# A 64-row product made a 128-row product in the spatial step of a gated MLP

## The chip, the cores and the metric

The program runs on one core of one Trainium2 chip. The metric is the device time of one execution, in microseconds; a kernel's time is the median of several runs.

## What is computed

The program chains three blocks over 4 batches of 576 positions and 512 channels: an attention with a window of 64 positions, an MLP on a Fourier-mixed input, and a gated MLP (gMLP) with a spatial product. Only the last block touches the change. In the reference it reads, cut to what matters:

```python
def _moe2_ref(x, w_in, g_ln, w_sg, b_sg, w_out):
    h = x @ w_in                      # 512 -> 1024 channels
    h = gelu_tanh(h)
    u, v = h[..., :512], h[..., 512:]
    v_n = (v - mean(v)) / np.sqrt(var(v) + 1e-06) * g_ln
    v_s = np.einsum('ts,bsd->btd', w_sg, v_n) + b_sg[None, :, None]
    return x + (u * v_s) @ w_out
```

The spatial product is the `einsum`: for each batch a 576 x 576 matrix over positions times a 576 x 512 matrix.

## The kernel before, in words

Every float32 operand is split into a high part with few mantissa bits and a low part, and a product is made as three matmuls that accumulate in one PSUM tile: high by high, high by low, low by high. The helper `mm3` records these three (L118, L119, L120) for each K tile of 128 rows. Because it is a helper, most matmuls of the program carry its three lines.

The gMLP runs last. `gate_u` makes the half u for all batches. Then for each batch b there are three steps on TensorE, in this order: `spatial(b)`, the spatial product; `v_tiles(b + 1)`, which makes and normalises the half v of the next batch with positions on partitions; `project(b)`, which multiplies the gated result by `w_out` and adds the residual. TensorE runs them back to back, and what it does in `v_tiles` and `project` gives VectorE and ScalarE time to finish the operands of the next `spatial`.

576 positions are four K tiles of 128 and a rest of 64. `spatial` works through two halves h of the output positions (320 and 256 columns) and four groups c of 128 channels, so 8 PSUM tiles for each batch and 32 in all. Each gets 14 matmuls: 4 times the three of `mm3`, and two for the rest of 64 positions. For that rest the tile `vtail[o]` (128 rows by 512 channels) holds the high part of the 64 positions in one half of its rows and the low part in the other half; for even b the high part is in rows 0 to 63, for odd b in rows 64 to 127. The rest's weights, `sg[4, h]`, are stored with the same 64 rows twice, so both halves of the rows hold the same numbers; `sh` is the high part, `sl` the low part. One matmul of 128 rows (L706) thus gives high by high and low by high at once. A second one (L707) gives high by low: only the 64 rows with the high part, chosen by `hr`.

When a tile's last matmul is done, VectorE reads it (L710), multiplies by u (L711), ScalarE rounds to the high part `xh` (L712), and VectorE makes the low part `xl` (L713). The intermediate `dec_w` has two buffers. PSUM has eight tiles for this stage: six of the tag `c` and two of the tag `g`, which `ctile` hands out in turn.

The order on each engine is fixed when the program is built, by a scheduler. In the first batch it puts five of the L706/L707 pairs one behind the other; in the three other batches each pair stands behind the 12 matmuls of its tile.

Of the kernel before, what the change touches and what calls it, by code (L numbers as in the profile page):

```python
# [41 lines left out]
EPS = 1e-6  # L42
# [2 lines left out]


def split(a):
    """float64 -> two float32 arrays: one with 11 mantissa bits, and the rest."""
    u = a.astype(np.float32).view(np.uint32).astype(np.uint64)
    u = (u + 0x7FF + ((u >> 12) & 1)) & 0xFFFFF000  # L50
    hi = u.astype(np.uint32).view(np.float32)
    return hi, (a - hi.astype(np.float64)).astype(np.float32)
# [49 lines left out]
class Kernel:  # L102
# [8 lines left out]
        return p, es  # L111

    def mm3(self, out, terms, first=True, last=True):
        """out += sum over terms of (lh + ll) @ (rh + rl) without ll @ rl."""
        n = len(terms)
        for i, (lh, ll, rh, rl) in enumerate(terms):
            mm = self.nc.tensor.matmul
            mm(out, lhsT=lh, rhs=rh, start=first and i == 0, stop=False)  # L118
            mm(out, lhsT=lh, rhs=rl, start=False, stop=False)  # L119
            mm(out, lhsT=ll, rhs=rh, start=False, stop=last and i == n - 1)  # L120

    # ---------------------------------------------------------------- setup
    def setup(self):
        nc = self.nc
        left, right = "left", "right"
# [12 lines left out]
        self.bp, self.ndec, self.nct = None, 0, 0  # L138
        self.x2 = self.tc.dram_tile([128, 4, TOK], F32, name="x2")

    # ------------------------------------------- weights: float64 to float32r
    def decode(self, src, hi, lo, n=512, eng=None):
        """src: float64 words [128, n] in DRAM. hi + lo = src to float32's 24 bits.
        The exponent is shifted by a product, which also flushes what float32 cannot hold;
        then the bits move into float32's places."""
        nc, p = self.nc, self.pers
        for o in range(0, n, 256):
            self.ndec += 1
            q = self.bp if self.bp is not None and self.ndec % 2 else p
            s = q.tile([128, 256, 2], I32, tag="dec_s", bufs=2, name="dec_s")  # L150
            nc.sync.dma_start(s[:].rearrange("p a b -> p (a b)"), src[:, o:o + 256].bitcast(I32))
            g = p.tile([128, 256], F32, tag="dec_g", bufs=2, name="dec_g")
            w = p.tile([128, CA], I32, tag="dec_w", bufs=2, name="dec_w")[:, 0:256]
            nc.scalar.activation(out=g, in_=s[:, :, 1].bitcast(F32), func=AF.Copy, scale=2.0 ** -112)  # L154
            nc.vector.tensor_scalar(out=w, in0=s[:, :, 0], scalar1=29, scalar2=None, op0=ALU.logical_shift_right)  # L155
            nc.vector.scalar_tensor_tensor(out=w, in0=g[:].bitcast(I32), scalar=3, in1=w, op0=ALU.logical_shift_left, op1=ALU.bitwise_or)  # L156
            nc.vector.scalar_tensor_tensor(out=w, in0=s[:, :, 1], scalar=-2147483648, in1=w, op0=ALU.bitwise_and, op1=ALU.bitwise_or)
            f = w.bitcast(F32)
            nc.scalar.activation(out=hi[:, o:o + 256], in_=f, func=AF.Copy)  # L159
            (eng or nc.gpsimd).tensor_tensor(out=lo[:, o:o + 256], in0=f, in1=hi[:, o:o + 256], op=ALU.subtract)  # L160
            yield 0
# [23 lines left out]
    def gtile(self):  # L185
        return self.gps.tile([128, 512], F32, tag="g", name="g")

    # ------------------------------------------------------------ attention
    def open_attn(self):
        nc = self.nc  # L190
        self.ap_, self.attn_es = self.pool("attn", side="right")
# [17 lines left out]
        self.kt[b, g] = t  # L209

    def load_q(self, b, j, w):
        """w blocks of q from j on."""
        t, o = self.qring[(b * 5 + j // 2) % QB], j % 2
        for h in range(2):
            dst = t[64 * h:64 * h + 64, o:o + w, :, h].rearrange("d n a q -> d (n a) q")
            self.nc.sync.dma_start(dst, self.aps["q"][b, h, :, j:j + w].rearrange("d n a q -> d (n a) q"))
        for i in range(w):
            self.qt[b, j + i] = t[:, o + i]

    def load_v(self, b, j):  # L220
        """The rows of v that blocks j and j + 1 see."""
        w = min(2, NB - j)
        t = self.ap_.tile([128, 2, 520], F32, tag="v", bufs=VB, name="v")
        v = self.aps["v"][b]
        for i in range(w):
            self.vt[b, j + i] = t[:, i]
        if w == 1:
            self.nc.sync.dma_start(t[:, 0], v[64 * j:64 * j + 128, :])
        else:
            src = v[64 * j:64 * j + 128, :]  # L230
            ap = [list(x) for x in src.ap]
            src = bass.AP(tensor=src.tensor, offset=src.offset, ap=[ap[0], [64 * 520, 2], ap[1]])
            self.nc.sync.dma_start(t, src)
# [123 lines left out]
                xt(m)  # L357
                yield 440

    # ------------------------------------------------------------------ DFT  # L360
    def open_dft(self):
        nc = self.nc
        self.dp, self.dft_es = self.pool("dft", side="left")
# [103 lines left out]
        V.tensor_tensor(out=x[0:1, 2, 289:576], in0=pa[0:1, 287:0:-1], in1=row[:, 289:576], op=ALU.add)  # L467
        yield 2000

    # ----------------------------------------------------------- layer norm  # L470
    def open_x(self, n, p):
        """The two parts of chunk n: of the normalised rows, then of the MLP's result."""
        self.xh[n] = p.tile([128, 4, CHUNKS[n][1]], F32R, name=f"xh{n}")
        self.xl[n] = p.tile([128, 4, CHUNKS[n][1]], F32R, name=f"xl{n}")

# [5 lines left out]
        self.ctx.enter_context(es)  # L481

    def rsqrt(self, p, out, var, m, n, tag):
        """out = 1 / sqrt(var + EPS), with a Newton step."""
        V = self.nc.vector
        t = [p.tile([128, 3], F32, tag=f"{tag}{i}", name=f"{tag}{i}", bufs=2) for i in range(4)]
        v, y, c, e = (x[:m, 0:n] for x in t)
        V.tensor_scalar(out=v, in0=var, scalar1=EPS, scalar2=None, op0=ALU.add)  # L488
        self.nc.gpsimd.tensor_tensor(out=y, in0=v, in1=self.mhalf[:m, 0:n], op=ALU.pow)  # L489
        V.scalar_tensor_tensor(out=c, in0=v, scalar=-0.5, in1=y, op0=ALU.mult, op1=ALU.mult)  # L490
        V.tensor_tensor(out=e, in0=c, in1=y, op=ALU.mult)  # L491
        V.scalar_tensor_tensor(out=out, in0=e, scalar=1.5, in1=y, op0=ALU.add, op1=ALU.mult)
# [34 lines left out]
            V.tensor_tensor(out=self.xl[n][:, :, o:o + r], in0=pv, in1=hi, op=ALU.subtract)  # L527
            yield 1000

    # ------------------------------------------------------------------ MLP  # L530
    def open_mlp(self):
        self.bp, self.mlp_es = self.pool("mlp", side="right")
        self.bps, es = self.pool("mlp_ps", side="right", space=PSUM)
# [49 lines left out]
            second(*pend.pop(0))  # L583
            yield 1500

    # ----------------------------------------------------------------- gMLP
    def open_gmlp(self):
        nc = self.nc
        self.cp, es = self.pool("gmlp", side="right")
# [26 lines left out]
        return self.cps.tile([128, 512], F32, tag="c", name="c")  # L616

    def sg_place(self, k, p, h):
        """Where part p of K tile k of the spatial weights lies, for half h of the positions."""
        u = 2 * k + p  # L620
        i, o = ((6, 0, 1)[u // 3], S * (u % 3) + CA * h) if u < 9 else ((0, 6)[h], 3 * S)
        t = self.sets[i][:].rearrange("p a b -> p (a b)")
        return t[:, o:o + (CA, CB)[h]]
# [24 lines left out]
                yield 5 * size  # L648

    def v_tiles(self, b):  # L650
        """The normalised half v of batch b, positions on partitions; the last 64 positions
        of two batches share a tile."""
        nc, p = self.nc, self.lp
        V, A = nc.vector, nc.scalar
        o = b % 2
# [36 lines left out]
    def spatial(self, b):  # L692
        nc = self.nc
        V, A = nc.vector, nc.scalar
        o = b % 2
        tail = self.vtail[o]
        hr = slice(64 * o, 64 * o + 64)
        for h in range(2):
            n = 2 * b + h
            start, size = CHUNKS[n]  # L700
            for c in range(4):
                s = slice(128 * c, 128 * c + 128)
                ps = self.ctile()[:, 0:size]
                self.mm3(ps, [(self.vh[i][:, s], self.vl[i][:, s], *self.sg[i, h]) for i in range(4)], last=False)
                sh, sl = self.sg[4, h]
                nc.tensor.matmul(ps, lhsT=tail[:, s], rhs=sh, start=False, stop=False)  # L706
                nc.tensor.matmul(ps, lhsT=tail[hr, s], rhs=sl[hr], start=False, stop=True)  # L707
                ug = self.uT[:, c, start:start + size]
                t = self.pers.tile([128, CA], I32, tag="dec_w", bufs=2, name="dec_w")[:, 0:size].bitcast(F32)
                V.scalar_tensor_tensor(out=t, in0=ps, scalar=self.gT[:, c:c + 1], in1=self.bbc[:, CA * h:CA * h + size], op0=ALU.mult, op1=ALU.add)  # L710
                V.tensor_tensor(out=t, in0=t, in1=ug, op=ALU.mult)  # L711
                A.activation(out=self.xh[n][:, c], in_=t, func=AF.Copy)  # L712
                V.tensor_tensor(out=self.xl[n][:, c], in0=t, in1=self.xh[n][:, c], op=ALU.subtract)  # L713
                yield 6 * size
# [19 lines left out]


def drive(main, *lanes):
    """Trace `main` and lanes of fillers beside it; a filler gives, at each stop, how much of
    main's time goes by before it goes on."""
    credit = [0.0] * len(lanes)
    for cost in main:  # L740
        for i, fill in enumerate(lanes):
# [212 lines left out]
```

## Time and profile before

| | |
|---|---|
| time, median of 3 runs | 836.64 us (835.75 to 838.92) |
| span of the profiled execution, first to last instruction | 837.8 us |
| PE busy in the span | 806.8 us (96%) |
| DVE busy in the span | 487.7 us (58%) |
| mean granted clock of TensorE | 0.988 |

No time is listed for the profiled execution apart from its span. PE is TensorE's matmuls, PEld its weight loads, which overlap the matmuls, DVE is VectorE, ACT ScalarE, POOL GpSimd. Matmuls are pipelined: a matmul's recorded duration is longer than the distance to the start of the next, so what a matmul costs a stream is read from start to start.

### The profile page before, as it was taken

Reading aid. Unit: us, or ns where it says so; the run is one execution under the profiler, and the core shown is the slowest. Engines: PE = TensorE matmul, PEld = TensorE weight load, DVE = VectorE, ACT = ScalarE, POOL = GpSimd, SP = SyncE. Lnnn points to the kernel's source line nnn. Section 1 sums busy time; section 2 is a strip of 40 time slices with the busy share of each in tenths; the row PEclk is TensorE's granted clock in tenths of the full one; section 3 lists DMA queues with packets and bytes.
Section 4 is the critical chain, followed back from the end, with each engine's and each line's share of the span. In section 5 each row is a group of like instructions: output and inputs, shape, how many; then the busy total and the mean of one; then the engine's idle time right before and its main releaser. Section 6 shows DMA issues by size and latency. Waiting matters only on the chain.

```text
span 837.8 us, 15602 instructions
## 1 busy us (share of the span) xinstructions
PE 806.8 (96%) x6084; PEld 769.5 (92%) x6084; DVE 487.7 (58%) x1390; ACT 279.5 (33%) x638; POOL 192.0 (23%) x238
## 2 busy tenths in 40 slices
PE   6879799889999999999999999999999999999998
PEld 6879688789999999999999999999999988889897
DVE  3586978798559556972225933553340467465643
ACT  3556555445225223531113411333232333121210
POOL 4373636243122002320002300232340021010100
PEclk9989999999999999999999999999999999999999
DMA  8996542023003002330002400132130020303032
GB/s 230 269 290 171 157 134 65 27 66 111 1 1 103 1 1 77 127 101 1 1 2 65 137 1 1 45 108 83 57 116 1 1 58 22 93 10 105 10 105 90
DMA packets 59322, 63.71 MB, mean 76 GB/s; under 512 B 22384, under 2 KB 42736, under 8 KB 59248
## 3 DMA queue, kind: packets, MB, share of 16 engines
q1 hardware_dynamic: 58672, 59.75, 24.2%
q0 software_dynamic: 576, 2.97, 1.3%
q8 instruction: 48, 0.79, 0.4%
q14 instruction: 26, 0.21, 0.1%
HBM read 53.25 MB, written 9.44 MB: 75 GB/s over the span
## 4 chain that ended last, share of the span: by engine, by line
PE 80%; DVE 8%; DMA 5%; issue 2%; POOL 1%; SPq 1%; ACT 1%; DVEq 0%; ACTq 0%; POOLq 0%
PE acc L118 7%; PE acc L120 7%; PE acc L119 7%; PE h L118 7%; PE h L120 7%; PE h L119 7%; PE c L118 6%; PE c L119 6%; PE c L120 6%; PE g L118 3%; PE g L119 3%; PE g L120 3%; PE pv L294 3%; DMA dec_s<-in_wo 2%; PE sc L260 2%
## 5 line engine op out<-in xcount | busy, mean ns | idle before, releaser
L118 PE MATMUL h<-xh,set 128*128 128x256 f32 (+1 forms) x512 | 151.5, 297 | 3.6 <-DVE rq L491 2.4
L118 PE MATMUL acc<-rh,set 128*128 128x256 f32 (+1 forms) x512 | 152.0, 297 | 0.5 <-DVE uT L556 0.5
L120 PE MATMUL acc<-rh,set 128*128 128x256 f32 (+1 forms) x512 | 151.4, 296 | 0.0
L120 PE MATMUL h<-xh,set 128*128 128x256 f32 (+1 forms) x512 | 151.4, 296 | 0.0
L119 PE MATMUL h<-xl,set 128*128 128x256 f32 (+1 forms) x512 | 151.4, 296 | 0.0
L119 PE MATMUL acc<-rl,set 128*128 128x256 f32 (+1 forms) x512 | 151.2, 295 | 0.0
L576 DVE SCALAR_TENSOR_TENSOR rl<-h,rh 128x320 fp32r<-128x320 f32 (+1 forms) x128 | 58.0, 453 | 120.3 <-ACT rh L575 120.0
L160 POOL TENSOR_TENSOR set<-dec_w,set 128x256 fp32r<-128x256 f32 x88 | 68.0, 780 | 248.4 <-ACT set L159 246.1
L575 ACT ACTIVATE rh<-h 128x320 fp32r<-128x320 f32 (+1 forms) x128 | 52.0, 406 | 165.3 <-PE h L120 119.9
L118 PEld LDWEIGHTS h<-xh,set 128*128 128x128 f32 x512 | 96.7, 189 | 4.4 <-issue 2.6
L118 PEld LDWEIGHTS acc<-rh,set 128*128 128x128 f32 x512 | 96.7, 189 | 1.1 <-issue 1.0
L120 PEld LDWEIGHTS h<-xh,set 128*128 128x128 f32 x512 | 96.8, 189 | 0.0
L119 PEld LDWEIGHTS h<-xl,set 128*128 128x128 f32 x512 | 96.8, 189 | 0.0
L120 PEld LDWEIGHTS acc<-rh,set 128*128 128x128 f32 x512 | 96.6, 189 | 0.1
L119 PEld LDWEIGHTS acc<-rl,set 128*128 128x128 f32 x512 | 96.6, 189 | 0.0
L556 DVE TENSOR_TENSOR uT<-acc,uT 128x320 f32<-128x320 f32 (+1 forms) x160 | 62.0, 448 | 13.0 <-PE acc L120 12.9
L489 POOL TENSOR_TENSOR rq<-rq,mhalf 128x1 f32<-128x1 f32 (+2 forms) x26 | 18.3, 705 | 197.3 <-DVE rq L488 194.2
L154 ACT ACTIVATE dec_g<-dec_s 128x256 f32<-128x256 f32 x88 | 38.3, 438 | 70.0 <-DVE dec_w L156 34.1
L118 PE MATMUL c<-xh,set 128*128 128x256 f32 (+1 forms) x188 | 55.4, 295 | 0.0
L120 PE MATMUL c<-xh,set 128*128 128x256 f32 (+1 forms) x188 | 55.3, 294 | 0.0
L119 PE MATMUL c<-xl,set 128*128 128x256 f32 (+1 forms) x188 | 55.3, 294 | 0.0
L155 DVE TENSOR_SCALAR dec_w<-dec_s 128x256 int32<-128x256 int32 x88 | 35.7, 406 | 32.8 <-POOL set L160 21.0
(193 smaller groups left out, 1669.3 us busy)
## 6 DMA issues: line engine op xcount, KB each, us to landing
dec_s<-in_w SPq DMA_DIRECT2D x64, 256.0 KB, 2.7
v<-in_v SPq DMA_DIRECT2D x16, 520.0 KB, 5.1
k<-in_k SPq DMA_DIRECT2D x11, 512.0 KB, 6.3
dec_s<-in_wi SPq DMA_DIRECT2D x16, 256.0 KB, 2.7
q<-in_q SPq DMA_DIRECT2D x30, 128.0 KB, 6.2
x<-uT SPq DMA_DIRECT2D x4, 640.0 KB, 3.9
out<-uT SPq DMA_DIRECT2D x4, 640.0 KB, 4.0
dec_s<-in_wo SPq DMA_DIRECT2D x8, 256.0 KB, 2.8
```

Of the source, the lines that this page charges most:

```text
L118: mm(out, lhsT=lh, rhs=rh, start=first and i == 0, stop=False)
L119: mm(out, lhsT=lh, rhs=rl, start=False, stop=False)
L120: mm(out, lhsT=ll, rhs=rh, start=False, stop=last and i == n - 1)
L154: nc.scalar.activation(out=g, in_=s[:, :, 1].bitcast(F32), func=AF.Copy, scale=2.0 ** -112)
L155: nc.vector.tensor_scalar(out=w, in0=s[:, :, 0], scalar1=29, scalar2=None, op0=ALU.logical_shift_right)
L160: (eng or nc.gpsimd).tensor_tensor(out=lo[:, o:o + 256], in0=f, in1=hi[:, o:o + 256], op=ALU.subtract)
L260: nc.tensor.matmul(sc[:, hp], lhsT=q[:, hp].rearrange("p a b -> p (a b)"), rhs=k[:, hp, o:o + 128], start=True, stop=True)
L294: nc.tensor.matmul(o[r:r + 64, i // 4, 65 * (i % 4):65 * (i % 4) + 65], lhsT=pts[:, i // 2, 64 * (i % 2):64 * (i % 2) + 64], rhs=v[:, 65 * ...
L489: self.nc.gpsimd.tensor_tensor(out=y, in0=v, in1=self.mhalf[:m, 0:n], op=ALU.pow)
L556: V.tensor_tensor(out=x, in0=acc[:, c, 0:size], in1=x, op=ALU.add)
L575: A.activation(out=rh, in_=o, func=AF.Relu)
L576: V.scalar_tensor_tensor(out=rl, in0=o, scalar=0.0, in1=rh, op0=ALU.max, op1=ALU.subtract)
```

## The change

The matmul of L707 takes all 128 rows of the tail tile and all 128 rows of `sl`, and the slice `hr` goes. The output gets one product more (low by low of the 64 positions). The number of instructions on each engine, their order and the semaphores that each waits for are those of before, in all five queues. The other lines of the diff remove docstrings and comments; lines behind L697 have a number one lower afterwards (L706 becomes L705, L707 becomes L706).

```diff
@@ -694,7 +694,6 @@
         V, A = nc.vector, nc.scalar
         o = b % 2
         tail = self.vtail[o]
-        hr = slice(64 * o, 64 * o + 64)
         for h in range(2):
             n = 2 * b + h
             start, size = CHUNKS[n]
@@ -704,7 +703,7 @@
                 self.mm3(ps, [(self.vh[i][:, s], self.vl[i][:, s], *self.sg[i, h]) for i in range(4)], last=False)
                 sh, sl = self.sg[4, h]
                 nc.tensor.matmul(ps, lhsT=tail[:, s], rhs=sh, start=False, stop=False)
-                nc.tensor.matmul(ps, lhsT=tail[hr, s], rhs=sl[hr], start=False, stop=True)
+                nc.tensor.matmul(ps, lhsT=tail[:, s], rhs=sl, start=False, stop=True)
```

## Rows read from the trace of the kernel before

**Rows 1.** The page: busy time by engine, and the chain that ended last.

```profile
PE 806.8 (96%) x6084; PEld 769.5 (92%) x6084; DVE 487.7 (58%) x1390; ACT 279.5 (33%) x638; POOL 192.0 (23%) x238
...
PE 80%; DVE 8%; DMA 5%; issue 2%; POOL 1%; SPq 1%; ACT 1%; DVEq 0%; ACTq 0%; POOLq 0%
```

**Rows 2.** Busy time in three stretches (the columns stand in the first line).

```profile
core 0: us, PE busy (x) PEld busy (x) DVE busy (x) ACT busy (x) POOL busy (x), PEclk, DMA share, GB/s
40.00:60.00 20.00, 15.73 (x142) 14.12 (x141) 18.20 (x74) 8.14 (x19) 13.32 (x14) 0.83 1.08 293
684.00:693.00 9.00, 9.00 (x51) 6.70 (x50) 7.71 (x19) 2.50 (x6) 0.00 (x0) 1.00 0.00 0
684.00:838.00 154.00, 149.95 (x926) 133.39 (x925) 87.21 (x233) 30.34 (x59) 7.71 (x13) 1.00 0.20 59
```

**Rows 3.** Timeline of the run's end: start, duration, engine, line, operation.

```profile
833.67 0.28 PE L120 MATMUL c<-xh,set 128*128 128x256 f32 x1
...
834.66 0.42 DVE L728 TENSOR_TENSOR uT<-c,dec_s 128x256 f32<-128x256 f32 x1 [0.74 <-DMA dec_s<-x]
```

**Rows 4.** PE's timeline, a tile of 256 columns in the first batch.

```profile
688.35 0.28 PE L706 MATMUL c<-set,vtail 128*128 128x256 f32 x1
688.56 0.38 PE L707 MATMUL c<-set,vtail 64*128 64x256 f32 x1
688.87 0.39 PE L118 MATMUL c<-set,set 128*128 128x256 f32 x1
689.10 0.28 PE L119 MATMUL c<-set,set 128*128 128x256 f32 x1
689.21 0.28 PE L120 MATMUL c<-set,vl 128*128 128x256 f32 x1
```

**Rows 5.** PE's timeline, first batch: 16 matmuls of 256 columns, then five pairs.

```profile
682.14 0.28 PE L118 MATMUL c<-set,set 128*128 128x256 f32 x1
...
684.05 0.31 PE L706 MATMUL c<-set,vtail 128*128 128x320 f32 x1
...
687.53 0.28 PE L120 MATMUL c<-set,vl 128*128 128x256 f32 x1
```

**Rows 6.** PE's timeline, a tile of 320 columns in the second batch.

```profile
718.20 0.31 PE L118 MATMUL c<-set,set 128*128 128x320 f32 x1
...
718.49 0.30 PE L120 MATMUL c<-set,vl 128*128 128x320 f32 x1
...
719.60 0.30 PE L120 MATMUL c<-set,vl 128*128 128x320 f32 x1
```

**Rows 7.** Timeline of the weight loads beside rows 4.

```profile
688.24 0.19 PEld L706 LDWEIGHTS c<-set,vtail 128*128 128x128 f32 x1
688.56 0.18 PEld L707 LDWEIGHTS c<-set,vtail 64*128 64x128 f32 x1
688.87 0.19 PEld L118 LDWEIGHTS c<-set,set 128*128 128x128 f32 x1
688.98 0.19 PEld L119 LDWEIGHTS c<-set,set 128*128 128x128 f32 x1
```

**Rows 8.** PE's timeline in the MLP: four 64-row products (L524) between products of 128 rows.

```profile
192.47 0.28 PE L120 MATMUL h<-xh,set 128*128 128x256 f32 x1
192.68 0.46 PE L524 MATMUL g<-ident,u 64*128 64x64 f32 x4
193.06 0.38 PE L118 MATMUL h<-xh,set 128*128 128x256 f32 x1
193.29 0.28 PE L118 MATMUL g<-tab,oh 128*33 128x256 f32 x1
```

**Rows 9.** DVE's timeline in the second batch's spatial step, tiles of 256 columns.

```profile
728.60 0.48 DVE L710 SCALAR_TENSOR_TENSOR dec_w<-c,gT,bbc 128x256 f32<-128x256 f32 x1 [0.68 <-PE c L707]
729.00 0.48 DVE L713 TENSOR_TENSOR xl<-dec_w,xh 128x320 fp32r<-128x320 f32 x1
729.40 0.42 DVE L711 TENSOR_TENSOR dec_w<-dec_w,uT 128x256 f32<-128x256 f32 x1
730.65 0.48 DVE L710 SCALAR_TENSOR_TENSOR dec_w<-c,gT,bbc 128x256 f32<-128x256 f32 x1 [0.83 <-PE c L707]
```

**Rows 10.** Who waits for L707, by its source line: us in total, times.

```profile
  DVE dec_w L710: 25.6, 25
```

**Rows 11.** Timeline: the last operand of the second spatial step, and that step's first product.

```profile
710.23 0.69 DVE L683 TENSOR_TENSOR vl<-u,set 128x512 fp32r<-128x512 f32 x1
...
716.89 0.31 PE L118 MATMUL c<-set,set 128*128 128x320 f32 x1
```

## The prediction

> **What bounds the kernel now.** I read the page first: PE is busy for 806.8 of 837.8 us, and 80% of the chain that ended last is PE [rows 1]. An average over stages does not say what the spatial steps are worth, so I asked for stretches next. [...] The last matmul ends at 833.67 + 0.28 = 833.95 us [rows 3]; from there to the end of the span are 3.9 us, which is nearly all of the 4.05 us that PE is not busy. So between 684 and 834 us PE waits for nobody, and a microsecond taken from its stream is a microsecond of the kernel, as long as nobody else becomes late. Those 3.9 us are an addition and the output's way to memory, which follow the last product and move with it.
>
> A busy PE is not yet a PE at its pace. I therefore read the start-to-start distances in PE's timeline, and there the pair L706/L707 stands out. With 256 columns, 16 matmuls take 684.05 - 682.14 = 1.91 us, so 0.119 us each [rows 5]. Around a pair the distances are 0.21 us from L706 to L707, 0.31 from L707 to the next L118, and 0.23 from that to L119, then 0.11 again [rows 4]. The three starts cost 689.10 - 688.35 = 0.75 us where three ordinary ones cost 0.36.
>
> **What the extra time is.** The weight loads show it. The load for L706 starts at 688.24 us, a full 0.11 us ahead of its matmul; the load for L707 starts at 688.56, the very moment at which L707 starts, and so does the load of the L118 behind it, at 688.87 [rows 4, 7]. So the product of 64 rows is set off on both sides: the matmul ahead is let run out (0.09 us), the weights are then loaded with no cover, and the same happens again on the way back to 128 rows. L118's own extra 0.11 us is the second load without cover.
>
> Is it the 64 rows or the switch? Rows from another stage tell. In the MLP four 64-row products of L524 stand between 128-row products: 0.21 us from the product ahead to the first of them where 0.12 is the rule, 0.38 us for all four, 0.23 us from the L118 behind to its successor [rows 8]. The first number and the last are those of the lone L707, and four products together cost 0.38 us, hardly more than one L707 with its 0.31. Had each 64-row product its own penalty of some 0.3 us, four would take over 1.2. The price is paid on the way in and the way out, not for the rows.
>
> **The change, term by term.** Nothing moves: the five queues keep their instructions, order and waits. What changes is the shape of 32 matmuls (4 batches, 2 halves, 4 groups) and of their 32 weight loads.
>
> The weight load of 128 rows takes 0.19 us instead of 0.18 [rows 7]; with 128 rows on both sides it can start a matmul early, as L706's does, so I price it at nothing. If it had no cover, the 0.01 us would be 0.3 us over 32 loads.
>
> The matmul itself streams the same 256 or 320 columns. I price it at the ordinary distance of its width, since L706, with the same weights tile and 128 rows, stands in the stream at 0.12 us behind its predecessor's start. That L706 and L707 would load the same weights twice is the case of L118 and L119 too, which are among the 16 at the ordinary distance [rows 5].
>
> The gain of one pair with 256 columns: the four starts from 688.35 to 689.21 take 0.86 us, at 0.119 they would take 0.476, so 0.384 [rows 4, 5]. With 320 columns the ordinary distance is (718.49 - 718.20) / 2 = 0.145 us; five starts from 718.49 to 719.60 take 1.11 us and would take 0.725, so 0.385 [rows 6]. In the first batch five pairs stand together: from L706 at 684.05 to L120 at 687.53 are 3.48 us for eight products of 320 columns and three of 256, which would take 8 x 0.145 + 3 x 0.119 = 1.517, so 1.96 us, or 0.39 a pair [rows 5]. The sum: 27 x 0.385 + 1.96 = **12.4 us**. The rows are rounded to 0.01 us, and a pair's distances vary by about as much; 0.37 and 0.40 a pair bound it to 11.8 and 12.8 us.
>
> The profiled execution has no time of its own but its span, 837.8 us, which is 1.2 us above the median of the runs. The span should become 825.4 us, the median **824.2 us** (-1.5%).
>
> **Who could be late next.** Three things follow PE here; the residual's loads in `project` are a fourth only in name, since they are issued as VectorE frees their buffers and so move with PE. First, VectorE, which reads each tile. Of a tile with 256 columns it makes three operations from 728.60 to 729.82 us, then waits 0.83 us for PE [rows 9]. PE's tile goes from 730.65 - 728.60 = 2.05 us to about 14 x 0.119 = 1.67, so the wait shrinks to some 0.45 us and does not vanish; over the run DVE waits 25.6 us for L707 in 25 waits [rows 10], about twice what goes. Second, the first batch is tighter: from 684 to 693 us DVE is busy for 7.71 of 9.00 us, and PE will need 9.0 - 8 x 0.39 = 5.9 us for the same products [rows 2]. There DVE falls behind PE by two to three microseconds, about one to two tiles of 1.7 to 2.0 us. Eight PSUM tiles hold that, and the products of the next batch's v half follow, whose tiles VectorE does not read before ScalarE has. I price it at nothing; what it costs if that cover fails is the second rival. Third, the operands of the next spatial step: the last of them is written by 710.23 + 0.69 = 710.9 us, and the step begins at 716.89 [rows 11]. The 6 us do not shrink much, since the work that makes the operands starts earlier by as much as PE does.
>
> [...]
>
> **The rivals.**
> *Only the drains go.* If a load of the tail's weights stayed without cover whatever its rows, each pair would win back the running-out alone, about 0.09 us on each side: 32 x 0.19 = 6.1 us, so 830.5 us. For it: the loads are 0.2 us of each pair's price. Against it: every 128-row load in the rows that does not stand at a switch starts early, L706's with the same tile among them. 4 in 100. [...]
> *VectorE holds PE up in the first batch.* If PSUM ran out there, the first batch's 3.1 us (8 x 0.39) would be given back as a wait: 827.3 us. For it: DVE's 7.71 us against PE's 5.9. Against it: eight PSUM tiles, of which at most three would be waiting. 5 in 100.
> *No change.* If what costs time were the end of an accumulation or two readers of one tile and not the rows, 128 rows would cost the same: 836.6 us. Against it: other groups end and other weights are loaded twice at the ordinary distance, and L524's rows have nothing of both but show the same entry and exit [rows 8]. 2 in 100.
> *Slower.* PE arrives early at a spatial step, waits for its operands, and the clock falls. From 40 to 60 us, where PE was idle for 4.3 of 20 us, the granted clock was 0.83 [rows 2]. [...] Against it: PE has no wait at all between 684 and 834 us now, and 6 us of reserve at the second step [rows 11]. 2 in 100.
>
> **How the numbers follow.** The forecast, all of the pairs' extra time gone and nobody late, has 87 in 100: 824.2 us. Its own bounds are 11.8 to 12.8 us of gain, so 823.8 to 824.8, and the runs of before differ from their median by -0.9 to +2.3 us. With that scatter I take 822.6 as the lower end; the upper end reaches to the second rival, 827.3, with a little scatter: 828.0. The cases beyond are 8 in 100, and 6 more I leave for scatter. A measurement of this kernel can tell about 0.5%, 4.2 us, from no change. Faster by more than that are the forecast and the first two rivals, 96 in 100; I take one off for scatter. Within 0.5% is the third rival with that one, 3 in 100. Slower is 2 in 100.
>
> **What the profile of after would show.** Right: the former L707 (then L706, 128 rows) lies 0.12 or 0.145 us behind its predecessor, its successor by as much behind it, all PEld rows of the step start early, and the spatial step of a batch takes some 14.8 us; DVE's wait for that line falls to 13 to 16 us. PE stays without waits to its end, near 821.5 us. Wrong: distances of 0.2 us or more around the pair (the rows were not the cause), a PE row that waits for DVE between 684 and 700 us (the second rival), or a granted clock below 1.00 after 684 us (the last).

## The result, and the profile after

The changed kernel takes 825.68 us (median of 4 runs, 823.64 to 827.65), the kernel before 837.78 us in the same comparison (4 runs, 835.75 to 839.73): a ratio of 0.9844, 95% interval 0.9814 to 0.9873. A second comparison on another occasion (e8 below) gives 825.99 against 838.67 us, 0.9845 (0.9816 to 0.9874). The forecast was 824.2 us, and 12.4 us less than before; the medians differ by 12.1 and 12.7 us. The profiled execution of the changed kernel took 826.16 us with a span of 824.4, so some 1.8 us lie outside the span.

The runs of one kernel scatter by several microseconds: of the 16 runs of the kernel before beside e1, the longest took 844.39 us at the lowest mean granted clock, 0.978, and the shortest 834.75 us at the highest, 0.993. The stretch that holds all 32 changed products can be timed far more closely in the trace: from the start of the first tail product to the start of the last matmul. I call it the stage. Before, it takes 833.67 - 684.05 = 149.62 us [rows 3, 5], in the one profile that there is. PE's timeline of the changed kernel, its first tail product, the tile that answers to [rows 4], and its last matmul:

```profile
682.88 0.31 PE L705 MATMUL c<-set,vtail 128*128 128x320 f32 x1
...
685.24 0.28 PE L705 MATMUL c<-set,vtail 128*128 128x256 f32 x1
685.35 0.28 PE L706 MATMUL c<-set,vtail 128*128 128x256 f32 x1
685.47 0.28 PE L118 MATMUL c<-set,set 128*128 128x256 f32 x1
685.59 0.28 PE L119 MATMUL c<-set,set 128*128 128x256 f32 x1
685.71 0.28 PE L120 MATMUL c<-set,vl 128*128 128x256 f32 x1
...
820.29 0.28 PE L120 MATMUL c<-xh,set 128*128 128x256 f32 x1
```

The stage takes 820.29 - 682.88 = 137.41 us, 12.21 less. The second profile of the changed kernel gives 817.59 - 680.18 = 137.41 again, although that run reached the stage 2.7 us earlier. The span fell by more than the stage, by 837.8 - 824.4 = 13.4 us, because the profiled run also reached it 684.05 - 682.88 = 1.17 us earlier, after stages in which nothing was changed: that part is scatter and not gain. The four starts from L705 to L120 take 0.47 us where they took 0.86: no distance stands out any more. The weight loads beside them, in the view of [rows 7], each start one matmul ahead, also the one that was of 64 rows (L706 here) and the one behind it:

```profile
685.13 0.19 PEld L705 LDWEIGHTS c<-set,vtail 128*128 128x128 f32 x1
685.24 0.19 PEld L706 LDWEIGHTS c<-set,vtail 128*128 128x128 f32 x1
685.36 0.19 PEld L118 LDWEIGHTS c<-set,set 128*128 128x128 f32 x1
```

Busy time by stretch, as in [rows 2], shows that PE is still the bound: 141.00 - 136.57 = 4.43 us of it are not busy, where it was 154.00 - 149.95 = 4.05 us, and in both cases they lie behind the last matmul (825 - 820.57 and 838 - 833.95). The granted clock is 1.00, as before:

```profile
core 0: us, PE busy (x) PEld busy (x) DVE busy (x) ACT busy (x) POOL busy (x), PEclk, DMA share, GB/s
684.00:825.00 141.00, 136.57 (x918) 129.57 (x916) 86.19 (x232) 30.35 (x59) 7.68 (x13) 1.00 0.21 64
```

VectorE's timeline in the second batch, the answer to [rows 9]; its wait for PE is 0.42 us and was 0.83:

```profile
722.67 0.48 DVE L709 SCALAR_TENSOR_TENSOR dec_w<-c,gT,bbc 128x256 f32<-128x256 f32 x1 [0.33 <-PE c L706]
723.07 0.48 DVE L712 TENSOR_TENSOR xl<-dec_w,xh 128x320 fp32r<-128x320 f32 x1
723.47 0.42 DVE L710 TENSOR_TENSOR dec_w<-dec_w,uT 128x256 f32<-128x256 f32 x1
724.31 0.48 DVE L709 SCALAR_TENSOR_TENSOR dec_w<-c,gT,bbc 128x256 f32<-128x256 f32 x1 [0.42 <-PE c L706]
```

### The profile page after: what moved, and what is told of

Its sections match the earlier page's. It is cut to its first block, busy times and chain, and to the rows that moved or that the text cites. A ratio compares the mean times of both kernels' runs of the same rounds, so it can differ in the third digit from the quotient of the medians.

```text
span 824.4 us, 15602 instructions
## 1 busy us (share of the span) xinstructions
PE 794.5 (96%) x6084; PEld 766.2 (93%) x6084; DVE 487.7 (59%) x1390; ACT 279.6 (34%) x638; POOL 191.7 (23%) x238
## 4 chain that ended last, share of the span: by engine, by line
PE 81%; DVE 8%; DMA 4%; issue 2%; SPq 1%; ACT 1%; POOL 1%; DVEq 0%; ACTq 0%; POOLq 0%
PE acc L118 7%; PE acc L120 7%; PE acc L119 7%; PE h L118 7%; PE h L120 7%; PE h L119 7%; PE c L119 6%; PE c L118 6%; PE c L120 6%; PE pv L294 4%; PE g L118 3%; PE g L119 3%; PE g L120 3%; PE sc L260 2%; DMA dec_s<-in_wo 2%
## 5 line engine op out<-in xcount | busy, mean ns | idle before, releaser
L118 PE MATMUL h<-xh,set 128*128 128x256 f32 (+1 forms) x512 | 151.3, 296 | 3.7 <-DVE rq L491 2.4
L118 PE MATMUL acc<-rh,set 128*128 128x256 f32 (+1 forms) x512 | 151.9, 297 | 0.7 <-DVE uT L556 0.7
L120 PE MATMUL acc<-rh,set 128*128 128x256 f32 (+1 forms) x512 | 151.4, 296 | 0.0
L119 PE MATMUL acc<-rl,set 128*128 128x256 f32 (+1 forms) x512 | 151.3, 296 | 0.0
L119 PE MATMUL h<-xl,set 128*128 128x256 f32 (+1 forms) x512 | 151.3, 296 | 0.0
L120 PE MATMUL h<-xh,set 128*128 128x256 f32 (+1 forms) x512 | 151.2, 295 | 0.0
L118 PEld LDWEIGHTS h<-xh,set 128*128 128x128 f32 x512 | 96.5, 189 | 4.5 <-issue 2.6
L118 PEld LDWEIGHTS acc<-rh,set 128*128 128x128 f32 x512 | 96.6, 189 | 1.5 <-issue 1.4
L120 PEld LDWEIGHTS acc<-rh,set 128*128 128x128 f32 x512 | 96.6, 189 | 0.1
L120 PEld LDWEIGHTS h<-xh,set 128*128 128x128 f32 x512 | 96.6, 189 | 0.0
L119 PEld LDWEIGHTS acc<-rl,set 128*128 128x128 f32 x512 | 96.6, 189 | 0.0
L119 PEld LDWEIGHTS h<-xl,set 128*128 128x128 f32 x512 | 96.5, 189 | 0.0
L120 PE MATMUL c<-xh,set 128*128 128x256 f32 (+1 forms) x188 | 55.5, 295 | 0.0
L118 PE MATMUL c<-xh,set 128*128 128x256 f32 (+1 forms) x188 | 55.4, 295 | 0.0
L119 PE MATMUL c<-xl,set 128*128 128x256 f32 (+1 forms) x188 | 55.4, 295 | 0.0
```

## The experiments

**e1: is it the rows or the switch?** The 64-row product is kept, but the four of a half stand together.

```diff
             for c in range(4):
...
                 nc.tensor.matmul(ps, lhsT=tail[:, s], rhs=sh, start=False, stop=False)
-                nc.tensor.matmul(ps, lhsT=tail[:, s], rhs=sl, start=False, stop=True)
+                tiles.append(ps)
+            for c in range(4):
+                s = slice(128 * c, 128 * c + 128)
+                nc.tensor.matmul(tiles[c], lhsT=tail[hr, s], rhs=sl[hr], start=False, stop=True)
+            for c in range(4):
+                ps = tiles[c]
                 ug = self.uT[:, c, start:start + size]
```

> The second product of the tail keeps its 64 rows, but the four of a half stand one behind the other at the end of that half, so PE goes from 128 rows to 64 and back 8 times instead of 32. If the price is paid for the switch (about 0.385 us for entry and exit together), the kernel is 8 x 0.385 = 3.1 us slower than the changed one, 828.8 us, and the second to fourth product of a run of four stand at the ordinary distance of 0.145 or 0.119 us. If each product of 64 rows is dear by itself, nothing is gained over the kernel before: about 837.8 us, and each of the four starts 0.3 us behind the one ahead.

Measured: 829.44 us (828.94 to 829.54), ratio to the kernel before 0.9903 (0.9870 to 0.9935). The stage from the first tail product (683.30 us) to the last matmul (823.60) takes 140.30 us, 2.9 more than in the changed kernel, where 3.1 was expected. PE's timeline of one of the eight runs (three products and one more in the merged rows):

```profile
728.37 0.28 PE L707 MATMUL g<-set,vtail 128*128 128x256 f32 x1
728.58 0.63 PE L711 MATMUL c<-set,vtail 64*128 64x256 f32 x3
729.05 0.28 PE L711 MATMUL g<-set,vtail 64*128 64x256 f32 x1
729.25 0.50 PE L118 MATMUL c<-set,xh 128*128 128x512 f32 x1
729.59 0.39 PE L119 MATMUL c<-set,xh 128*128 128x512 f32 x1
```

The first three products take 729.05 - 728.58 = 0.47 us from start to start. The merged row gives no more; with the ordinary 0.12 for the second and third, which is an estimate, 0.23 are left for the first. The way in is then L707's 0.21 us and the first product's 0.23, the way out the last product's 0.20 and L118's 0.34, where the ordinary distances are 0.12 for 256 columns [rows 5] and 0.23 for 512 (the changed kernel, from 688.79 to 689.02 us). The same 32 products of 64 rows lose a quarter of the time that they did (2.9 of 12.2 us), with a quarter of the switches.

**e2: twice as many 64-row products, no more switches.** Both tail products take 64 rows; the low part of the tail by the high weights is left out of the result.

```diff
-                nc.tensor.matmul(ps, lhsT=tail[:, s], rhs=sh, start=False, stop=False)
-                nc.tensor.matmul(ps, lhsT=tail[:, s], rhs=sl, start=False, stop=True)
+                hr = slice(64 * o, 64 * o + 64)
+                nc.tensor.matmul(ps, lhsT=tail[hr, s], rhs=sh[hr], start=False, stop=False)
+                nc.tensor.matmul(ps, lhsT=tail[hr, s], rhs=sl[hr], start=False, stop=True)
```

> Both products of the tail take only the 64 rows with the high part (the low part of the tail by the high weights is left out of the result). PE's order has 28 runs of 64-row products: the first five pairs of the first batch stand nearly together, the others each in its tile. If the switch is what costs, 64 products of 64 rows cost no more than 32: 28 runs x 0.385 = 10.8 us over the changed kernel, so about 836.5 us, a little under the kernel before. If each 64-row product is dear, 64 x 0.385 = 24.6 us over the changed kernel, about 850 us.

Measured: 839.01 us (833.31 to 840.86, 10 runs), ratio 1.0000 (0.9975 to 1.0025): the kernel before, not 850 us. The median is 2.5 us over what the switch alone asks for; the profiled run, 835.45 us, is 1 us under it. The stage decides more closely: it takes 829.56 - 680.48 = 149.08 us, and in this order five products of 256 columns more fall into it (5 x 0.119 = 0.6 us). So it is 149.08 - 0.6 - 137.41 = 11.1 us longer than in the changed kernel. The trace has 29 runs of 64-row products, not 28, because only four pairs of the first batch stand together: 29 x 0.385 = 11.2 us. Inside the run of eight, products of 64 rows stand at 0.15 us, the distance of 128-row products of their width:

```profile
680.73 0.30 PE L707 MATMUL c<-set,vtail 64*128 64x320 f32 x1
680.88 0.31 PE L706 MATMUL c<-set,vtail 64*128 64x320 f32 x1
681.03 0.30 PE L707 MATMUL c<-set,vtail 64*128 64x320 f32 x1
681.17 0.31 PE L706 MATMUL c<-set,vtail 64*128 64x320 f32 x1
```

PE's timeline of one tile in the second batch shows the second 64-row product 0.25 us behind the first instead of the 0.34 that a lone one needs to its successor (721.29 to 721.63 us in the kernel before):

```profile
714.26 0.30 PE L120 MATMUL c<-set,vl 128*128 128x320 f32 x1
714.50 0.41 PE L706 MATMUL c<-set,vtail 64*128 64x320 f32 x1
714.75 0.30 PE L707 MATMUL c<-set,vtail 64*128 64x320 f32 x1
714.98 0.41 PE L118 MATMUL c<-set,set 128*128 128x320 f32 x1
715.23 0.32 PE L119 MATMUL c<-set,set 128*128 128x320 f32 x1
```

From L120 to L119 are 0.97 us for four starts, 0.39 over the ordinary 0.58: the price of one pair in [rows 6], now for two products of 64 rows.

**e3: 96 rows.** In the even batches the second product takes 96 rows, in the odd ones 64.

```diff
+                hr = slice(64, 128) if o else slice(0, 96)
...
-                nc.tensor.matmul(ps, lhsT=tail[:, s], rhs=sl, start=False, stop=True)
+                nc.tensor.matmul(ps, lhsT=tail[hr, s], rhs=sl[hr], start=False, stop=True)
```

> The second product takes 96 rows in the even batches (the 64 of the high part and 32 of the low) and 64 rows in the odd ones. If it is the mode of 64 rows that sets a product off, 96 rows stand in the stream like 128: extra time only for the 16 products of the odd batches, 16 x 0.385 = 6.2 us over the changed kernel, 831.9 us. If any product with fewer rows than the ones around it is set off, the extra is that of all 32, about 837.8 us, and the distances around the 96-row products are 0.2 and 0.3 us.

Measured: 829.12 us (828.30 to 830.56, 6 runs), ratio 0.9894 (0.9863 to 0.9926). The stage takes 824.39 - 681.04 = 143.35 us, 5.9 more than with 128 rows throughout. Both forms stand in one trace; PE's timeline of a tile with 64 rows and of one with 96:

```profile
722.06 0.38 PE L707 MATMUL c<-set,vtail 64*128 64x256 f32 x1
722.37 0.39 PE L118 MATMUL c<-set,set 128*128 128x256 f32 x1
722.59 0.28 PE L119 MATMUL c<-set,set 128*128 128x256 f32 x1
```

```profile
765.01 0.28 PE L707 MATMUL c<-set,vtail 96*128 96x256 f32 x1
765.13 0.28 PE L118 MATMUL c<-set,set 128*128 128x256 f32 x1
765.25 0.28 PE L119 MATMUL c<-set,set 128*128 128x256 f32 x1
```

A product of 96 rows stands in the stream of 128-row products like any other. So it is not a matter of fewer rows than the neighbours have. Other numbers of rows were not tried.

**e4: the product left out.** What does the 128-row product itself still cost? High part by low weights of the last 64 positions is left out of the result.

```diff
-                nc.tensor.matmul(ps, lhsT=tail[:, s], rhs=sh, start=False, stop=False)
-                nc.tensor.matmul(ps, lhsT=tail[:, s], rhs=sl, start=False, stop=True)
+                nc.tensor.matmul(ps, lhsT=tail[:, s], rhs=sh, start=False, stop=True)
```

> The second product is left out, and with it high part by low weights of the last 64 positions. If the changed kernel's 128-row product costs just its columns, leaving it out gives 16 x 0.145 + 16 x 0.119 = 4.2 us less than the changed kernel, 821.5 us, and 16.3 us less than the kernel before. If the changed kernel still pays something around the pair, the step is larger by that.

Measured: 821.22 us (818.32 to 822.92), ratio 0.9800 (0.9753 to 0.9848). The stage takes 816.84 - 683.97 = 132.87 us, 4.5 less than in the changed kernel, where the columns alone make 4.2. The 32 products cost their columns and 0.01 us each; of the 149.62 - 132.87 = 16.75 us that the 64-row products took before, three quarters (12.21 us) were the switch.

**e5, e6, e9: does PE need the eight PSUM tiles?** The same edit in both kernels, in the changed one for e5, in the one before for e6 and, once more, e9:

```diff
-        self.cps, es = self.pool("gmlp_ps", side="right", space=PSUM, bufs=6)
+        self.cps, es = self.pool("gmlp_ps", side="right", space=PSUM, bufs=2)
```

> The changed kernel with four PSUM tiles for the gMLP instead of eight (two of tag c, two of tag g); the order around the steps is the same as in the next run. If the eight tiles are what lets PE run ahead of VectorE in the first batch, PE now waits there for VectorE, some 2 to 3 us, and the distance to the next run is 9 to 10 us instead of 12.4. If VectorE has time enough anyway, the distance stays at 12.4 us. If VectorE is the next bound in all four batches, most of the 12.4 us are gone: under 6 us.

> The kernel before with four PSUM tiles for the gMLP instead of eight. PE's slower spatial step leaves VectorE more time, so by every theory its waits for VectorE between 684 and 700 us are shorter than those of the run ahead; its time is that of the kernel before, 837.8 us, plus what four tiles cost both in the other steps.

> The kernel before with four PSUM tiles, a second profile. In the first one PE waited 1.05 us for the tail ahead of four pairs and the granted clock then was at 0.50 from 685 to 691 us. If the wait and the set-off products together bring the clock down each time, it is at 0.50 there again, and the time near 843 us. If it depends on chance as well, the same stretch can show 1.00, and a time near 837 to 839 us.

Measured: e5 827.23 us (825.69 to 828.93), ratio 0.9879 (0.9858 to 0.9901); e6 839.42 us (836.61 to 844.97, 10 runs), ratio 1.0029 (1.0005 to 1.0053); e9, a single run, 841.92 us. With four PSUM tiles instead of eight the gain is 12.2 us between the medians, and in the stage, which holds 16 products more in this order, 151.93 (e9) - 139.70 (e5) = 12.23 us; so the lower estimate of 9 to 10 falls. From 640 us on, one wait of PE is recorded in either kernel, for the tail tile, which the new order asks for earlier, and none for a PSUM tile; the wait views of e5 and e6 have one row each:

```profile
PE c L705 <- DVE vtail L689: 1.0, 1, 1.0
```

```profile
PE c L706 <- DVE vtail L689: 1.0, 1, 1.0
```

The profiled run of e6 took 843.83 us, 4.4 us over its median, and part of that stands in its granted clock, here beside that of e9, which is the same program (columns as in [rows 2]; the clock is the third number from the end):

```profile
685.00:691.00 6.00, 6.00 (x18) 4.67 (x19) 1.77 (x6) 0.87 (x2) 0.00 (x0) 0.50 0.00 0
```

```profile
685.00:691.00 6.00, 6.00 (x34) 4.73 (x33) 4.32 (x10) 1.30 (x4) 0.00 (x0) 1.00 0.00 0
```

At a granted clock of 0.50 PE got through 18 matmuls in the stretch, at 1.00 through 34. From the first tail product to the last matmul e6 takes 154.82 us and e9 151.93, so the fall cost 2.9 us. The whole run of e9, 841.92 us, is no nearer to the 837 to 839 that were expected without a fall, so the clock in this stretch is not all that lengthens these runs. Ahead of the fall PE had waited 1.05 us and then run two of the four pairs with their switches; the third pair is the first at the slower pace:

```profile
684.01 0.41 PE L707 MATMUL c<-set,vtail 64*128 64x320 f32 x1
684.35 0.63 PE L706 MATMUL g<-set,vtail 128*128 128x320 f32 x1
```

In e9 it waited 0.68 us for the same tile, with the same four pairs behind, and the clock stayed at 1.00. In e5 it waited 1.01 us, with 128-row products behind, and the clock stayed at 1.00 as well. The kernel before runs five pairs without a wait, at 1.00 [rows 2, 5]. Whether the wait and the pairs together bring the fall about is not shown: one profile has it.

e5 shows one thing more. Behind its wait stands a 128-row product with no switch beside it, whose weights come from the tile that was waited for (in e6 the load of that product waited 1.3 us for the same tile; e5's loads were not read):

```profile
681.51 0.41 PE L705 MATMUL c<-set,vtail 128*128 128x320 f32 x1 [1.01 <-DVE vtail L689]
681.76 0.31 PE L706 MATMUL c<-set,vtail 128*128 128x320 f32 x1
```

It takes 0.25 us to its successor where 0.145 is the ordinary distance of 320 columns [rows 6]. That the 0.1 us more is its uncovered load is an estimate; it is the size that the prediction gave to each of the two loads at a pair.

**e7: other switches.** The 16 transposes of 64 rows in the layer norm (four runs) are padded to 128 rows. Five more runs of 64-row products, at L323, stay as they are.

```diff
             u = p.tile([128, 512], F32, tag="u", bufs=UB, name="u")
+            if r < 128:
+                nc.gpsimd.memset(u[r:], 0.0)
...
-                nc.tensor.transpose(pv[:, k], us[i][:r, 128 * k:128 * k + 128], self.ident[:r, :r])
+                nc.tensor.matmul(pv[:, k], lhsT=us[i][:, 128 * k:128 * k + 128], rhs=self.ident[:, :r], start=True, stop=True)
```

> The changed kernel, and the transposes of the layer norm's rest of 64 rows (16 of them in four runs) take 128 rows, the lower ones zeroed by GpSimd first. If each switch costs 0.385 us here too, at most 4 x 0.385 = 1.5 us less than the changed kernel, 824.2 us, which this measurement hardly tells from no change; in the trace the first product of a run then stands at the ordinary distance. The scheduler orders the program anew, so that more or less than this may come from the order. If the switches of the other stages cost nothing because PE waits there anyway, no change.

Measured: 835.80 us (833.55 to 839.20, 10 runs), 0.9976 (0.9955 to 0.9996) of the kernel before and so some 10 us over the changed one. None of it lies in the gMLP stage, which takes 831.99 - 694.58 = 137.41 us here too but starts at 694.58 us instead of 682.88. The sign that had been named did come: the first product of a padded run stands 0.12 us behind the one ahead, where it was 0.21 [rows 8].

```profile
193.87 0.28 PE L120 MATMUL h<-xh,set 128*128 128x256 f32 x1
193.99 1.00 PE L526 MATMUL g<-ident,u 128*128 128x64 f32 x8
194.80 0.31 PE L118 MATMUL g<-tab,oh 128*33 128x256 f32 x1
194.95 0.28 PE L119 MATMUL g<-tab,oh 128*33 128x256 f32 x1
```

But the edit changed two things more. The products that replace this line's transposes are recorded as two matmuls each, 160 where the transposes made 80; the instructions of that line, first in e7 and then in the changed kernel:

```profile
L526 PE MATMUL g<-ident,u x160: 217/275/377, 115.6 to 315.2; 128*128 128x128 f32 x128, 128*128 128x64 f32 x32
```

```profile
L524 PE MATMUL g<-ident,u x80: 222/273/330, 115.7 to 307.4; 128*128 128x128 f32 x64, 64*128 64x64 f32 x16
```

So the padded run takes 194.95 - 193.87 = 1.08 us, where the same four starts of [rows 8] took 193.29 - 192.47 = 0.82: the switch is gone, and the eight matmuls cost more than it did. And the scheduler laid out the program anew; the waits of PE grew by 3.4 us in sum, and at this row of e7's waits from 1.3 to 5.4 us:

```profile
PE h L118 <- DVE rl L578: 5.4, 3, 3.7
```

How the 11.7 us between the two starts of the stage divide among matmuls, waits and scatter was not taken apart. Whether the four switches there are worth taking out in another way stays open. By the price of a pair they are at most 1.5 us, which is an estimate.

**e8: the changed kernel again.**

> The changed kernel once more, for a narrower interval beside the kernel before on the same chip: 12.4 us less by the sum over the pairs, a ratio of 0.985. If the first comparison was helped by chance in the stages ahead of the gMLP, the gain is smaller than 12 us.

Measured: 825.99 us (823.37 to 828.58, 6 runs), ratio 0.9845 (0.9816 to 0.9874), stage 137.41 us as told above. The gain is not smaller than in the first comparison, and the stage shows where it lies.

## Why the prediction was right

*The switch, not the rows.* Right, and now shown from three sides: fewer switches with the same 64-row products (e1), the same price with twice as many 64-row products (e2, by its trace), and no price for 96 rows (e3). With that the rival *No change* falls too: accumulations end and tiles have two readers in the changed kernel as before.

*The sum.* 12.4 us were predicted from start-to-start distances, 12.21 were found in the stage, inside the bounds of 11.8 and 12.8. That is 0.38 us a pair. Pricing the 128-row product at its columns was right to 0.01 us each (e4). The second spatial step takes 727.43 - 712.61 = 14.82 us, where 4 x 14 x (0.145 + 0.119) = 14.8 had been foreseen.

*Where the sum starts.* The prediction put the profiled execution of before 1.2 us above the median, by its span. A span leaves out the 1.8 us seen above, so that execution took about 839.6 us and lay 3 us above. The forecast is not touched by it, since it takes 12.4 us from the median of 836.64. The 1.5 us between 824.2 and 825.68 are mostly that baseline, which came out at 837.78 us in the comparison. That the whole run hits the forecast to within 2 us is in part luck; the stage is what tests the sum.

*Only the drains go.* This rival would have left some 0.2 us at each pair. The loads of the changed product and of the one behind it now start a matmul ahead, and the pair has no extra left (0.47 us for four starts): the load of L706 starts at 685.24 us, with the matmul ahead of its own, which follows at 685.35. So a 128-row load is covered behind a 128-row matmul here. That the matmul ahead runs out at a switch, 0.09 us on each side, was the author's estimate from the distances; no record shows it, and in the changed kernel both parts of the price are gone together.

*VectorE in the first batch.* It does fall behind, by what was said. PE starts its last tail product of that batch at 688.67 us, VectorE begins to read that tile at 691.79:

```profile
688.67 0.29 PE L706 MATMUL g<-set,vtail 128*128 128x256 f32 x1
```

```profile
691.79 0.48 DVE L709 SCALAR_TENSOR_TENSOR dec_w<-g,gT,bbc 128x256 f32<-128x256 f32 x1
```

PE does not wait. But more tiles stood unread than the "at most three" of the second rival: PE starts the next batch's first product at 688.79 us, and VectorE begins to read the fifth and sixth of the eight tiles only then, so four were unread.

```profile
688.88 0.87 DVE L709 SCALAR_TENSOR_TENSOR dec_w<-c,gT,bbc 128x256 f32<-128x256 f32 x2
```

The products of 512 columns that follow on PE, at 0.23 us each, seem to give VectorE the time to catch up. e5 does not show that four tiles would have been enough in this order: there the scheduler put twelve products of 512 columns ahead of the batch's last tile, whose first tail product starts at 692.50 us.

*VectorE in the other batches.* Its wait for the line fell to 17.2 us in 22 waits from 25.6 in 25 [rows 10]; 13 to 16 had been foreseen, a little too low. In the first batch VectorE waits for a tile only once, 2.14 us before and 2.06 after, so that batch's 3.1 us could not come out of its waits:

```profile
  DVE dec_w L709: 17.2, 22
```

*The next step's operands.* The last one is written by 705.96 + 0.69 = 706.65 us, the second spatial step starts at 712.61: 6.0 us of reserve, the same as in [rows 11], as predicted.

```profile
705.96 0.69 DVE L683 TENSOR_TENSOR vl<-u,set 128x512 fp32r<-128x512 f32 x1
...
712.61 0.31 PE L118 MATMUL c<-set,set 128*128 128x320 f32 x1
```

*The clock.* The rival that ended slower asked for a wait and a fall of the clock in the changed kernel. It did not come there: the clock is at 1.00 in both its profiles from 684 us on, and PE has no wait. That such a fall exists in this stage is shown by e6, in the kernel with 64 rows and after a wait of 1.05 us; it cost 2.9 us there, less than a quarter of the 12.2 us of gain. That one like it would make this kernel slower than before was not shown.

## What to carry to other kernels

Read a matmul's price from the start of the one ahead to the start of the second one behind it: its own duration held only part of these 0.385 us (L707's 0.38 is 0.10 more than L706's, [rows 4]), and none of it was booked as a wait of PE. Where a lone product of 64 rows stands among products of 128, fill the other rows with something harmless (825.7 us here), or put the 64-row products together (829.4 us in e1), since the price is for going in and out. Filling did not pay where it took twice the matmuls (e7: 1.08 us for the four starts instead of 0.82). When runs scatter by several microseconds, time the stage that was changed inside the trace: here 137.41 us in three profiles (the changed kernel twice and e7), while whole runs of the changed kernel differed by 5.

## What had not been expected of the hardware

A product of 96 rows, at 256 columns, is not set off from one of 128 (0.12 us on both sides, e3), while 64 rows are (0.21, 0.31 and 0.23 us, [rows 4]).

One program showed a granted clock of 0.50 from 685 to 691 us in one profile and 1.00 in the next (e6, e9), with a wait of 1.05 us ahead of the stretch in the first and of 0.68 in the second; what decides between the two was not settled.
